# Shifting the layer norm and a convolution branch against a gated MLP's matmuls on one core

## The chip, the cores and the metric

The kernel runs on one core of one Trainium2 chip. The metric is device microseconds (us) of that core; lower is better. Five engines work side by side: TensorE (PE in the profile; PEld is its weight load), VectorE (DVE), ScalarE (ACT), GpSimd (POOL) and SyncE (SP), which issues most of the transfers.

## The reference, cut to what matters

The program computes a forward pass and all its gradients. `x` is 2048 x 1024 in bf16, normed row by row; the normed `xn` feeds two branches that are added.

```python
def _fwd_reference(...):
    def _A_ref(q, k, v, shift_k, ssm_k, ssm_D):          # the convolution branch
        k_shift = sum of k_pad[:, t:t + S] * shift_k[:, ks - 1 - t]   # ks = 4 taps per channel (a loop, condensed)
        kv = k_shift * v
        y = irfft(rfft(kv padded) * rfft(ssm_k padded))[:S]           # long convolution per channel, condensed
        y = y + kv * ssm_D
        return q * y
    def _B_ref(x, W_gate, W_up, W_down):                 # the MLP, F = 3584
        gate = x @ W_gate; up = x @ W_up                 # condensed
        h = relu(gate) * up
        return h @ W_down
    x = A_q
    xn = _layernorm(x)
    return x + _A_ref(xn, A_k, ...) + _B_ref(xn, B_W_gate, ...)

def reference(...):
    out, vjp = jax.vjp(_fwd_reference, ...)
    return (out, *vjp(grad_out))                         # 10 outputs
```

## The kernel before

The MLP's 512-column matmuls, "large" below, are the bulk of TensorE's work. The first phase, `hidden`, goes through fourteen blocks: seven blocks of weight columns for each half of the rows. The norm of the 16 row tiles is a generator that the first blocks advance by `chunk()`. The convolution branch is a second generator, `steps()`, with eight groups of 128 channels. The driver counts the planned nanoseconds of MLP work and advances the branch when its counter reaches zero: `A_START` sets when it begins, and each `yield n` says how much MLP work to lay between this step and the next.

```python
    a_steps, left = a.steps(), A_START            # A_START = 45_000
    for pace, phase in mlp():
        for ns in phase:                          # 1730 per group of 8 large matmuls
            left -= ns * pace
            while a_steps is not None and left <= 0:
                d = next(a_steps, None)
                ...
                left += d
```

The head of the branch loads the first group and writes a small table of the four taps to memory and back, to spread it over all partitions:

```python
    def steps(self):
        sk_t = self.shift_rows()          # taps transposed by TensorE
        self.pin = True
        nx = self.loads_1(0)              # hn (filter), gt (gradient), sD
        self.loads_2(nx)                  # kp (k), vt (v)
        yield 10000
        self.load(self.sk_d, sk_t[:])     # store of the tap table
        yield 13000
        self.load_taps(nx)                # reload into skb, one row for all partitions
        yield 9500
        self.load_xn(nx)                  # xt, the normed input
        ...
        for gi in range(self.NG):
            for p, d in self.slots(st, gi):   # p: TensorE's part, d: VectorE's
                self.run(p); self.run(d)
                yield self.SLOT               # 1760
```

A group's slots begin with the taps (`tk`: `ksh` and `tap` from `kp` and `skb`, on VectorE) beside the filter's first matmuls (`f1h`), then the product gt*xt, the flip of the filter (`flH`, a VectorE transpose) and its second matmuls (`f2H`):

```python
        tk = self.taps(st, ksh, kp, [(3, 0), (2, 1), (1, 2), (0, 3)])
        f1h = self.fwd1_filter(st)
        f1g = self.fwd1(st, "Bg", gt)
        yield f1h, tk if gi == 0 else None
        yield f1h, tk
        yield None, self.both(lambda: self.add_D(st), tk)
        yield None, (lambda: self.gate_grad(st)) if gi == 0 else tk
        yield None, tk
        flH = ...
        yield f1g, flH
        ...
```

In the MLP, what VectorE does after each product of the `up` weights frees the PSUM bank (TensorE's output buffer) for a later group, and stands in the same queue as the taps:

```python
                ps = self.ps_tile("ps_u")
                self.gemm8(ps, xT[s], wu, mid)
                self.pri.pin(nc.vector.scalar_tensor_tensor(out=ru[s][:, 1, :], ..., in1=ps[:], ...))
                self.pri.pin(nc.vector.tensor_tensor(out=ht[:], ...))
```

## Time and profile before

| | before |
|---|---|
| median, lowest and highest of 3 runs | 1912.05, 1912.03, 1914.49 us |
| the run that left the profile | 1915.21 us, span 1912.6 us, mean granted clock 0.998 |
| TensorE busy | 1898.4 us, 99% |
| the two waits of TensorE above 2 us | 3.18 us (copy of a tile), 2.14 us (gt*xt) |

A span runs from the core's first to its last instruction and is some 2 us shorter than the time.

One more view of before matters later, SyncE's timeline around the head of the branch (start, duration, instruction):

```profile
72.70 0.53 SPq L88 DMA_DIRECT2D sk_d<-sk_t  x1
...
73.77 4.45 SPq L88 DMA_DIRECT2D hn<-in_A_ssm_k_dram  x2
...
82.72 3.80 SPq L88 DMA_DIRECT2D kp<-in_A_k_dram  x4
86.56 1.40 SPq L88 DMA_DIRECT2D vt<-in_A_v_dram  x2
...
95.19 0.44 SPq L88 DMA_DIRECT2D skb<-sk_d  x1
```

The table's store goes out at 72.70, ahead of the group's own loads, which take SyncE from 73.77 to 87.96 only to issue; the reload goes at 95.19, and the first filter matmul is at 97.67 us. In the code the store is called behind the loads, but the program as built issues it in front of them, so the order of issue has to be read from the trace. In VectorE's timeline the first tap product then waits little for the table:

```profile
99.70 1.23 DVE L80 TENSOR_TENSOR ksh<-kp,skb 128x2048 bf16<-128x2048 bf16 x1 [0.72 <-DMA skb<-sk_d]
```

### The profile page before, as it was taken

The page shows a single profiled execution, that of the slowest core. Times are in us where ns is not written, and L with a number is a line of the kernel's source. Part 1 is how long each engine was busy: PE and PEld are TensorE (multiplying, and loading weights), DVE is VectorE, ACT ScalarE, POOL GpSimd, SP SyncE. Part 2 cuts the span into 40 slices and gives each one's busy share as a digit, 9 for nine tenths or more (in the row PEclk, how much of TensorE's full clock was granted, in tenths as well). Part 3 has the DMA queues.
Part 4 walks back from the last instruction along what each step waited for, and adds up shares of the span by engine and source line. Part 5 has one row for each costly group of instructions (what it writes and reads, how often), then busy time and mean ns, then how long its engine had stood idle before and what let it go on. Part 6 is the DMA issues. An engine that isn't in the chain of part 4 may idle for free.

```text
span 1912.6 us, 36039 instructions
## 1 busy us (share of the span) xinstructions
PE 1898.4 (99%) x15447; PEld 872.8 (46%) x15447; DVE 908.9 (48%) x1355; ACT 617.7 (32%) x858; POOL 15.0 (1%) x37
## 2 busy tenths in 40 slices
PE   8999999999999999999999999999999999999999
PEld 3444444444444444444444444444444544444444
DVE  6767767767767754543444444410122232222222
ACT  5854354354354344344344344311000000000000
POOL 1000000000000000000000000000000000000000
PEclk9999999999999999999999999999999999999999
DMA  9975688985784882655662633385999965555553
GB/s 244 264 190 147 171 189 185 221 191 135 182 192 134 248 232 78 171 134 183 159 172 80 174 100 122 102 244 184 255 246 239 231 159 121 121 121 121 121 121 72
DMA packets 692640, 323.13 MB, mean 169 GB/s; under 512 B 524024, under 2 KB 663040, under 8 KB 692480
## 3 DMA queue, kind: packets, MB, share of 16 engines
q1 hardware_dynamic: 681984, 299.99, 63.9%
q10 hardware_dynamic: 9216, 16.65, 2.9%
q0 software_dynamic: 1280, 4.20, 0.6%
q8 instruction: 120, 1.97, 0.4%
q14 instruction: 40, 0.33, 0.1%
HBM read 143.79 MB, written 95.44 MB: 125 GB/s over the span
## 4 chain that ended last, share of the span: by engine, by line
PE 97%; DMA 1%; DVE 1%; ACT 0%; SPq 0%; issue 0%; DVEq 0%; ACTq 0%
PE ps_x L1275 20%; PE ps_w L1048 20%; PE ps_u L799 10%; PE ps_h L799 10%; PE ps_o L1206 10%; PE ps_g L799 10%; PE ps_d L1048 9%; PE ps L72 6%; PE ps_d L1061 1%; PE ps_w L1061 1%; DMA ln_x<-in_A_q_dram 1%; DMA xt<-xn_d 0%; PE ps_r L1236 0%; DMA wu<-in_B_W_up_dram 0%; PE pst_x L831 0%; ACT ln_j L727 0%
## 5 line engine op out<-in xcount | busy, mean ns | idle before, releaser
L1048 PE MATMUL ps_w<-ugs,xn_nat 128*128 128x512 bf16 x1728 | 382.9, 379 | 0.0
L799 PEld LDWEIGHTS <-xnT 128*128 128x128 bf16 x1792 | 170.6, 98 | 214.9 <-issue 13.5
L1048 PEld LDWEIGHTS <-xn_nat 128*128 128x128 bf16 x1728 | 164.6, 98 | 200.6 <-issue 7.1
L799 PE MATMUL ps_g<-wg,xnT 128*128 128x512 bf16 x896 | 207.0, 382 | 3.9 <-DVE xnT L834 3.5
L799 PE MATMUL ps_u<-wu,xnT 128*128 128x512 bf16 x896 | 208.0, 382 | 0.2
L799 PE MATMUL ps_h<-wdT,goT 128*128 128x512 bf16 x896 | 205.6, 379 | 0.0
L1293 ACT ACTIVATE w<-xn,m 128x512 f32<-128x512 bf16 x32 | 24.3, 806 | 553.0 <-issue 317.2
L1275 PE MATMUL ps_x<-wgT,ggT 128*128 128x512 bf16 x896 | 198.6, 379 | 0.0
L1275 PE MATMUL ps_x<-wuT,guT 128*128 128x512 bf16 x896 | 198.6, 379 | 0.0
L1206 PE MATMUL ps_o<-wd,hT 128*128 128x512 bf16 (+1 forms) x896 | 187.6, 372 | 0.0
L1048 PE MATMUL ps_d<-g_nat,hs 128*128 128x512 bf16 x768 | 171.5, 379 | 0.0
L1275 PEld LDWEIGHTS <-guT 128*128 128x128 bf16 x896 | 87.7, 98 | 105.7
L1275 PEld LDWEIGHTS <-ggT 128*128 128x128 bf16 x896 | 87.7, 98 | 105.5
L1206 PEld LDWEIGHTS <-hT 128*128 128x128 bf16 x896 | 87.7, 98 | 100.0
L799 PEld LDWEIGHTS <-goT 128*128 128x128 bf16 x896 | 85.1, 98 | 104.1 <-issue 4.5
L302 DVE STREAM_TRANSPOSE flp<-C 128x1024 f32<-128x1024 f32 x48 | 90.4, 1932 | 84.9 <-ACT C L76 84.9
L902 DVE SCALAR_TENSOR_TENSOR ru<-ru,ps_u 128x512 bf16<-128x512 bf16 x112 | 76.5, 683 | 109.2 <-issue 37.1
L965 ACT CAST gh<-ps_h 128x512 bf16<-128x512 f32 x112 | 65.4, 584 | 178.4 <-PE ps_h L799 158.1
L76 ACT CAST C<-ps 128x1024 bf16<-128x1024 f32 x96 | 92.5, 1015 | 77.2 <-PE ps L72 76.3
L1152 ACT CAST wi<-ps_w 128x512 bf16<-128x512 f32 x108 | 63.8, 590 | 161.2 <-PE ps_w L1048 149.7
L1048 PEld LDWEIGHTS <-hs 128*128 128x128 bf16 x768 | 72.6, 98 | 89.5 <-issue 5.0
L1277 DVE CUSTOM_DVE_ANT_0 gx<-ps_x,gy 128x512 f32<-128x512 f32 x32 | 22.1, 691 | 182.1 <-PE ps_x L1275 182.1
(160 smaller groups left out, 1494.5 us busy)
## 6 DMA issues: line engine op xcount, KB each, us to landing
ug_d<-ru SPq DMA_DIRECT2D x112, 256.0 KB, 3.3
ugs<-ug_d SPq DMA_DIRECT2D x112, 256.0 KB, 5.1
wg<-in_B_W_gate_dram SPq DMA_DIRECT2D x56, 256.0 KB, 4.2
wu<-in_B_W_up_dram SPq DMA_DIRECT2D x56, 256.0 KB, 5.0
h_d<-ht SPq DMA_DIRECT2D x112, 128.0 KB, 2.3
hs<-h_d SPq DMA_DIRECT2D x56, 256.0 KB, 5.4
out_dram<-wi SPq DMA_DIRECT2D x56, 256.0 KB, 2.6
gt<-in_grad_out_dram SPq DMA_DIRECT2D x32, 256.0 KB, 5.0
```

The lines of the kernel that those rows point to most:

```text
L72: self.pri.pin(self.nc.tensor.matmul(out, lhsT=lhsT, rhs=rhs, start=start, stop=stop))
L76: self.pri.pin(self.nc.scalar.copy(out=out, in_=in_))
L302: self.pri.pin(self.nc.vector.transpose(out=df[:, c0:c0 + 32, :], in_=sf[:, c0:c0 + 32, :]))
L799: self.pri.pin(self.nc.tensor.matmul(ps[:], lhsT=xT[:, kt * P:(kt + 1) * P], rhs=w(kt), start=(kt == 0), stop=(kt == self.DT - 1)), always ...
L902: self.pri.pin(nc.vector.scalar_tensor_tensor(out=ru[s][:, 1, :], in0=ru[s][:, 0, :], scalar=0.0, in1=ps[:], op0=ALU.is_gt, op1=ALU.mult))
L965: self.pri.pin(nc.scalar.copy(out=gh[:], in_=ps[:]))
L1048: self.pri.pin(self.nc.tensor.matmul(ps[:], lhsT=lhsT(st), rhs=rhs(st), start=(st == 0), stop=(st == self.ST - 1)))
L1061: self.pri.pin(self.nc.tensor.matmul(ps[i][:], lhsT=lhsT(i, st), rhs=rhs(i, st), start=(st == 0), stop=(st == self.ST - 1)))
L1152: self.pri.pin(nc.scalar.copy(out=wo[0][:, d, :], in_=ps[:]))
L1206: nc.tensor.matmul(ps, lhsT=hT[:, kt, :], rhs=self.wd[:, kt, oc], start=(kt == 0), stop=(kt == self.FT - 1))
L1275: nc.tensor.matmul(ps, lhsT=T[:, kt, :], rhs=W[:, kt, oc], start=(i == 0), stop=(i == n - 1))
L1293: nc.scalar.activation(out=w[:, oc], in_=xn[:, oc], func=ACT.Identity, scale=m[:, 7:8], bias=m[:, 6:7])
```

## The change

Its intent is to take away TensorE's waits near the start. Part 1: the norm of tiles 6 and 7 goes behind the copies of tiles 4 and 5 in VectorE's queue. Part 2: the norm of tiles 12 to 15 moves to the second block, and so the whole branch starts later, since it needs all of xn. With it the first group's order is new, and the distances in the head of `steps()` are halved. Part 3: from group 3 on, the tail of a group carries the head of the next.

```diff
@@ steps(): the head of the branch
         nx = self.loads_1(0)
         self.loads_2(nx)
-        yield 10000
+        yield 5000
         self.load(self.sk_d, sk_t[:])
-        yield 13000
+        yield 5000
         self.load_taps(nx)
-        yield 9500
+        yield 7000
         self.load_xn(nx)
 ...
-A_START = 45_000
+A_START = 80_000
@@ slots(): the first group's order, and mixed borders (cut)
+    MERGED = 3
 ...
+        if gi == 0:
+            yield None, flH
+            yield None, flH
+            yield None, tk
+            yield f2H, tk
+            yield None, None
+            yield f2H, lambda: self.gate_grad(st)
+            yield f1g, None
 ...
+        if self.MERGED <= gi and not last:
+            nx = st["nx"]
 ...
+            self.begin(nx)
+            yield ib, nx["tk"]
+            yield nx["f1h"], nx["tk"]
 ...
@@ hidden(): the norm (cut)
+            def flip_ahead(sp):
+                flip(min(sp + 6, HS))
+                if sp == 0:
+                    with self.tc.issue_after(self.copied.ins):
+                        chunk()
 ...
                 yield from first_gate_up(2)
-                chunk()
 ...
-                if ahead and sp in (2, 4):
-                    chunk()
-                if n == 1 and sp < 4:
+                if n == 1 and sp in (0, 2):
+                    with self.tc.issue_after(self.stored.ins):
+                        load(8 + sp // 2)
+                if ahead and sp == 4 or n == 1 and sp != 2:
                     chunk()
```

## The prediction

> **What bounds the kernel now.** I read the page first, then the waits of TensorE, then the timeline around each of them, then busy time and clock by stretch. From the page:
>
> ```profile
> PE 1898.4 (99%) x15447; PEld 872.8 (46%) x15447; DVE 908.9 (48%) x1355; ACT 617.7 (32%) x858; POOL 15.0 (1%) x37
> PEclk9999999999999999999999999999999999999999
> ```
>
> TensorE is busy 1898.4 of 1912.6 us. The order listing of both kernels has the same instructions on every engine, form by form (30,896 rows on TensorE, 1,357 on VectorE, 892 on ScalarE, 1,043 on SyncE). So the change removes no work: what it can gain is TensorE's idle time, 1912.6 - 1898.4 = 14.2 us, and whatever TensorE loses while it counts as busy. The waits of TensorE (engine, line and releaser: us in total, times, longest):
>
> ```profile
> PE ps_g L799 <- DVE xnT L834: 3.5, 2, 3.2
> PE ps L72 <- DVE gt L80: 2.1, 1, 2.1
> PE pst_x L831 <- DVE ln_x L781: 1.7, 2, 1.5
> PE ps_warm L845 <- POOL warm L842: 1.5, 1, 1.5
> PE ps L72 <- ACT B L76: 0.9, 2, 0.5
> ```
>
> Two waits stand out: 3.2 us for the copy of a transposed tile, 2.1 us for the product of gradient and normed input. The 1.5 us waits belong to the start, which the change leaves alone, and some 2.6 us lie after the last matmul (it ends near 1910). The timeline shows both big waits and what follows them (start, duration, instruction, idle before it):
>
> ```profile
> 30.07 1.03 PE L799 MATMUL ps_h<-wdT,goT 128*128 128x512 bf16 x4
> 34.28 5.31 PE L799 MATMUL ps_g<-wg,xnT 128*128 128x512 bf16 x16 [3.18 <-DVE xnT L834]
> ...
> 109.80 0.61 PE L72 MATMUL ps<-gt,R 64*128 64x512 bf16 x4 [2.14 <-DVE gt L80]
> 110.33 5.31 PE L799 MATMUL ps_u<-wu,xnT 128*128 128x512 bf16 x16
> ```
>
> Sixteen matmuls after each wait take 5.31 us by the timeline; by the chain they take 5.31 and 5.25 where later groups of 16 take 3.45. So each wait is paid twice. The windows view (busy us, granted clock last but two) says why:
>
> ```profile
> 31.10:34.28 3.18, 0.00 (x0) 0.00 (x0) 2.48 (x7) 2.63 (x6) 0.00 (x0) 1.00 1.17 233
> 34.28:39.60 5.32, 5.32 (x17) 2.07 (x18) 3.02 (x10) 1.88 (x5) 1.07 (x2) 0.68 1.03 242
> 107.66:109.80 2.14, 0.00 (x2) 0.01 (x2) 1.29 (x2) 0.60 (x1) 0.00 (x0) 1.00 0.86 243
> 110.40:115.65 5.25, 5.25 (x19) 1.88 (x20) 3.94 (x5) 1.78 (x2) 0.00 (x0) 0.68 0.72 151
> ```
>
> The clock is whole during the idle stretch and 0.68 in the stretch after it: 5.32 us x (1 - 0.68) = 1.70 us lost.
>
> Why the first wait: VectorE's timeline.
>
> ```profile
> 28.30 0.42 DVE L904 TENSOR_TENSOR ht<-ru 128x512 bf16<-128x512 bf16 x1
> 31.73 0.17 DVE L745 TENSOR_SCALAR ln_b<-ln_s 128x2 bf16<-128x2 f32 x1 [3.02 <-ACT ln_j L727]
> 31.94 0.17 DVE L752 CAST ln_s<-ln_b 128x2 f32<-128x2 bf16 x1
> 32.14 0.88 DVE L756 TENSOR_SCALAR ln_x<-ln_x,ln_s 128x1024 bf16<-128x1024 bf16 x2
> 32.94 0.68 DVE L966 TENSOR_TENSOR ru<-ru,gh 128x1024 bf16<-128x1024 bf16 x1
> 33.55 1.28 DVE L834 COPY xnT<-pst_x 128x1024 bf16<-128x1024 bf16 x2
> ```
>
> VectorE idles 3.02 us in front of the norm of tiles 6 and 7, whose input lands late (the chain has that load from 22.30 for 7.13 us), while the copies of tiles 4 and 5 (their transposes run on TensorE from 29.18 for 1.06 us) stand behind it in the queue.
>
> **What the Trainium skill says.** "TensorE: Matmul & The Clock Gate", section "Part 1: The HAM clock gate": the clock is halved after an idle window of about 3.4 us, the window runs freely, and about 3.4 us of activity restores it. The trace agrees on the cost (1.7 us is half of 3.4) but not on the length: 2.14 us of idle were enough here, while 1.51 us at 8.3 us were not. The same page, "Architectural detail", says that VectorE and ScalarE work their queues strictly in order; the blocked copies are that. "Perfetto Trace Analysis", section "What 'DMA-bound' means", names an issuing sequencer that is solid DMA slices as one form of DMA limit; SyncE's timeline from 29.24 to 52.05 us is that, with gaps under 0.2 us.
>
> **The change part by part.** (1) In the changed order on VectorE the two copies of tiles 4 and 5 stand before the norm of 6 and 7, and on ScalarE the first evacuation of ps_h before its sums. Worked through with the durations above: ht ends 28.72; ps_h of the first tile ends about 28.4, its cast (0.58) about 29.0, the product 29.7, copies 30.4 and 31.0. TensorE comes to ps_g at 31.10. The 3.18 us go, and with them 5.31 - 3.45 = 1.86 us of slow clock: **-5.0**. The norm of 6 and 7 still hangs on the load (29.47), so it ends near 37.5 as before; TensorE now wants these tiles at 31.0 + 32 x 0.216 + 12 x 0.216 = 40.5. Covered by 3 us.
>
> (2) The convolution starts later: before, its first matmul stands behind 361 large matmuls, now behind 457, 96 x 0.216 = 20.7 us later by order. In group 0 the product gt*xt now has its place eleven slots after the load of xt (a slot is 8 large matmuls, 1.73 us), where it had four, about 7 us, against a load that the chain shows from 101.59 for 6.80 us. The second wait goes, 2.14 + (5.25 - 3.45): **-3.9**.
>
> (3) The norm of tiles 12 to 15 moves to the second block. xt needs all of xn. By counts, the last tile's scaling ends near 107 us, its store lands some 5.4 us later (the median of such stores from 22 to 70 us), and xt is issued near 97.67 + 20.7 - 5 = 113. Just covered; no gain in itself.
>
> (4) From group 3 on, the tail of a group carries the head of the next. A group then takes 544 or 560 large matmuls instead of 600, so the branch ends behind 5,025 large matmuls, not 5,057, in spite of the late start. The loads for the output phase come no later. Where the old group 4 began, two pairs of filter matmuls stood only 2 large ones apart at 682.9 us and waited 0.35 + 0.52 us for ScalarE; now they stand 16 apart: **-0.9**.
>
> (5) What it adds. In group 0 the second stage of the filter (f2H) comes one slot sooner, 64 large matmuls and 8 filter ones after the first: 64 x 0.216 + 2 x 0.54 = 14.9 us. VectorE's list up to the second flip, with its durations (5 tap operations of 1.22; two flips of 1.94; bias 0.54; two pairs of 0.69 and 0.42; two gradient products of 0.69) comes to 14.1 us, begins about 1.3 us after the first filter matmul and has about 0.5 us of gaps: 16.0. TensorE would wait 1 us: **+1.1**, too short to slow the clock, if 1.51 was.
>
> (6) After (1) TensorE comes 5 us sooner to the second block's weights. SyncE was issuing without a gap up to these, so their load will not move 5 us: I put it at 51.4 instead of 52.05 (one 0.4 us load no longer precedes it). With the median landing of 4.2 us and four issues over 2.7 us, pieces land from 55.6 to 58; TensorE wants them from 56.1 to 57.4. **+0.5**, an estimate between 0 and 1.5; likewise **+0.2** for tighter places in group 0 (the flip of the gradient and its second stage meet to within 0.2 us).
>
> Sum: -5.0 - 3.9 - 0.9 + 1.1 + 0.5 + 0.2 = -8.0. From the median, 1912.05 - 8.0 = **1904.0 us**, 0.4% less.
>
> **The rivals.** (a) The waits come back elsewhere: TensorE, 5 to 9 us ahead, meets late weights at 56 us (DMA share 0.99 to 1.07 of 16 engines from 48 to 60 us) or at the third block, and one gap of 2 us costs another 1.7 us of clock. For it: SyncE's gapless issue, and near 539 us a late weight load already costs about 0.7 us. Against it: the change takes one 512 KB load and four 256 KB stores of xn out of that stretch, and moves the convolution's first loads behind the third block's weights. If it wins at both places: 1907 to 1910. (b) VectorE becomes the bound in the mixed tails. Against it: before, VectorE is busy 36 of 50 us in the first phase but 19 to 26 in the second, and mixing begins at the seam between them, so even 10% more leaves half of it free. If wrong, a microsecond in each of five tails: 1909. (c) The whole 9 us plus the small waits go and nothing returns: 1902. (d) The later start pushes the branch past the output phase: +20 us, but the counts in (4) exclude it.
>
> **Range and chances.** Floor and ceiling are close: removing every idle microsecond and both slow stretches gives 1912 - 14.2 - 3.7 = 1894, so 2% (1873.8) is out of reach for a change without fewer instructions. The base runs lie within 2.5 us. Small returns are likelier than none, so the range leans up: 1901.0 to 1908.5. Faster by 2%: 0.01; same: 0.985; slower: 0.005.
>
> **What would show it.** Right: no wait of ps_g for xnT above 0.5 us, none of ps for gt, the granted clock whole after the first 7 us, TensorE's busy time down by about 3.7 us and idle by about 4.5. Step 5: a wait of ps for flp near 1 us around 128 us. Step 6: the first ps_g after 56 us waiting on wg. Wrong: a third slow stretch of the clock, or waits of TensorE on casts in the tails of groups 3 to 7, or a gap before the output phase.

## The result, and the profile after

The kernel after took 1914.96 us in the median of four runs (1913.69 to 1918.04), against 1912.17 (1912.03 to 1914.49) for before: ratio 1.0014, 95% interval 0.9997 to 1.0031. A ratio here is the mean time of one kernel's fast runs over that of the other's in the same rounds, so not quite the ratio of the medians quoted. Within 2%, "same" was right; the predicted gain of 8 us did not come, and the time lies above the range of 1901.0 to 1908.5.

The head of the page of after:

```profile
span 1911.9 us, 35799 instructions
...
PE 1879.4 (98%) x15217; PEld 872.8 (46%) x15447; DVE 909.8 (48%) x1355; ACT 618.3 (32%) x858; POOL 15.0 (1%) x37
```

It must not be read against before's 1898.4. This trace lacks 230 of the 15,447 matmul records, and the waits view lists 70 gaps of up to 0.2 us that "waited for nothing", where before's complete trace has none. The waits that have a releaser can be compared (engine, line and releaser: us in total, times, longest):

```profile
PE ps_g L835 <- DVE ru L939: 3.2, 1, 3.2
...
...
PE ps_g L835 <- DMA wg<-in_B_W_gate_dram: 0.7, 2, 0.5
PE ps_u L835 <- DMA wu<-in_B_W_up_dram: 0.6, 2, 0.3
```

Both big waits of before are gone. The wait for the tile copy is down to 0.3 us in the whole span, and in TensorE's timeline the product that had waited 3.18 us follows with no gap, at full speed:

```profile
30.30 3.62 PE L835 MATMUL ps_g<-wg,xnT 128*128 128x512 bf16 x15
```

The new waits lie together, 90 us later. TensorE's timeline there (the bracket is the idle time in front):

```profile
119.08 1.89 PE L835 MATMUL ps_g<-wg,xnT 128*128 128x512 bf16 x8
124.18 3.57 PE L835 MATMUL ps_g<-wg,xnT 128*128 128x512 bf16 x8 [3.21 <-DVE ru L939]
...
135.73 0.75 PE L72 MATMUL ps<-flp,FW 64*32 64x128 bf16 x64 [1.67 <-DVE flp L302]
```

Eight products take 1.89 us in front of the wait and 3.57 behind it. The windows view (us, busy times, then granted clock, DMA share, GB/s) shows why:

```profile
120.97:124.18 3.21, 0.00 (x1) 0.00 (x0) 1.84 (x3) 0.60 (x1) 0.00 (x0) 0.83 1.17 177
124.18:132.30 8.12, 8.12 (x25) 3.09 (x25) 8.04 (x10) 0.60 (x1) 0.00 (x0) 0.65 0.80 196
```

The clock is 0.65 over 8.12 us of work: 8.12 x 0.35 = 2.84 us lost. With the two waits that makes 3.21 + 2.84 + 1.67 = 7.7 us.

What TensorE waited for is an evacuation (`ru`), so the next view is VectorE's timeline:

```profile
113.59 0.43 DVE L941 TENSOR_TENSOR ht<-ru 128x512 bf16<-128x512 bf16 x1
122.31 1.23 DVE L80 TENSOR_TENSOR ksh<-kp,skb 128x2048 bf16<-128x2048 bf16 x1 [8.29 <-DMA skb<-sk_d]
123.45 0.68 DVE L939 SCALAR_TENSOR_TENSOR ru<-ru,ps_u 128x512 bf16<-128x512 bf16 x1
```

VectorE stands idle for 8.29 us in front of the first tap product, for the tap table (0.72 us in before). The evacuation that TensorE needs is next in the queue and cannot pass. And the table is late because of SyncE:

```profile
99.43 4.78 SPq L88 DMA_DIRECT2D hn<-in_A_ssm_k_dram  x2
...
109.12 4.52 SPq L88 DMA_DIRECT2D kp<-in_A_k_dram  x4
113.69 1.31 SPq L88 DMA_DIRECT2D vt<-in_A_v_dram  x2
...
115.91 0.56 SPq L88 DMA_DIRECT2D sk_d<-sk_t  x1
...
119.13 0.33 SPq L88 DMA_DIRECT2D skb<-sk_d  x1
```

The same eleven loads as before take 99.43 to 115.00 to issue, but now the table's store comes after them, at 115.91, and its reload at 119.13, when the store has landed. The first filter matmul is at 112.71, so the branch begins before its table has even been stored. In before the three yields laid 10 + 13 + 9.5 = 32.5 us of MLP work between the loads and the first slot; now it is 5 + 5 + 7 = 17 us, of which the issue alone eats 15.6.

### The profile page after: what moved, and what is told of

The parts are those of the page before. It is cut to its first block, busy times and chain, and to the rows that moved or that the text cites. A ratio compares the mean times of both kernels' runs of the same rounds, so it can differ in the third digit from the quotient of the medians.

```text
span 1911.9 us, 35799 instructions
## 1 busy us (share of the span) xinstructions
PE 1879.4 (98%) x15217; PEld 872.8 (46%) x15447; DVE 909.8 (48%) x1355; ACT 618.3 (32%) x858; POOL 15.0 (1%) x37
## 4 chain that ended last, share of the span: by engine, by line
PE 95%; DMA 2%; issue 1%; SPq 1%; DVE 1%; ACT 0%; DVEq 0%
PE ps_x L1319 20%; PE ps_w L1092 19%; PE ps_o L1250 10%; PE ps_u L835 9%; PE ps_h L835 9%; PE ps_g L835 9%; PE ps_d L1092 9%; PE ps L72 6%; PE ps_d L1105 1%; SPq L88 1%; PE ps_w L1105 1%; DMA wu<-in_B_W_up_dram 1%; DMA wg<-in_B_W_gate_dram 1%; PE ps_r L1280 0%; DVE flp L302 0%
## 5 line engine op out<-in xcount | busy, mean ns | idle before, releaser
L1092 PE MATMUL ps_w<-ugs,xn_nat 128*128 128x512 bf16 x1673 | 375.5, 379 | 5.7 <-issue 4.1
L1092 PE MATMUL ps_d<-g_nat,hs 128*128 128x512 bf16 x741 | 167.4, 379 | 3.2 <-issue 2.7
L835 PEld LDWEIGHTS <-goT 128*128 128x128 bf16 x896 | 84.9, 98 | 104.6 <-issue 5.7
```

The costliest lines, as they stand in the source:

```text
L835: self.pri.pin(self.nc.tensor.matmul(ps[:], lhsT=xT[:, kt * P:(kt + 1) * P], rhs=w(kt), start=(kt == 0), stop=(kt == self.DT - 1)), always ...
L1092: self.pri.pin(self.nc.tensor.matmul(ps[:], lhsT=lhsT(st), rhs=rhs(st), start=(st == 0), stop=(st == self.ST - 1)))
```

## The experiments

Eleven kernels ran (before and after again among them), all correct, each five times. The main theory (A) was that the late table in the head of the branch eats the gain. Its rivals, by the letters of the expectations: VectorE has too much work in group 0 whenever it starts (B), the loss lies in late weights for the second and third blocks (C), the gain of part 1 is eaten by late loads anyway (D), the mixed borders cost the time (E), the profile of before was of an unlucky run, so that there was less to gain (F).

| run | median (us) | ratio to before | 95% interval |
|---|---|---|---|
| after (first measured) | 1914.96 | 1.0014 | 0.9997 to 1.0031 |
| e1_taps_early | 1909.98 | 0.9987 | 0.9973 to 1.0001 |
| e2_taps_behind | 1908.52 | 0.9978 | 0.9966 to 0.9991 |
| e3_norm67_only | 1912.67 | 1.0004 | 0.9992 to 1.0017 |
| e4_no_mixing | 1915.5 | 1.0016 | 1.0004 to 1.0029 |
| b_again | 1912.77 | 0.9997 | 0.9985 to 1.0010 |
| a_again | 1916.02 | 1.0013 | 1.0000 to 1.0025 |
| e5_table_and_order | 1906.21 | 0.9963 | 0.9950 to 0.9975 |
| e9_conv_part_only | 1910.0 | 0.9982 | 0.9968 to 0.9995 |
| e10_cured_old_norm | 1907.83 | 0.9977 | 0.9963 to 0.9991 |
| e11_lead_restored | 1909.48 | 0.9986 | 0.9974 to 0.9999 |
| e12_cured_no_mixing | 1907.03 | 0.9971 | 0.9958 to 0.9983 |

Before, beside them, had medians of 1912.34 (the first four experiments), 1913.0 (the next four) and 1912.66 us (the last three).

**e1: the table early.** After, with the tap table stored and reloaded ahead of the group's loads.

```diff
+        yield 4000
+        self.load(self.sk_d, sk_t[:])
+        yield 4000
+        first = dict(gi=0)
+        self.load_taps(first)
         nx = self.loads_1(0)
+        nx.update(first)
         self.loads_2(nx)
-        yield 5000
-        self.load(self.sk_d, sk_t[:])
-        yield 5000
-        self.load_taps(nx)
+        yield 10000
         yield 7000
-A_START = 80_000
+A_START = 72_000
```

> Changed kernel with the tap table stored and reloaded ahead of the first convolution loads, all else as it was. Theory A (VectorE's queue stood 8.3 us behind the first tap product, which waited for the tap table; TensorE then waited 3.2 us for a bank, ran 6.8 us at half clock and waited 1.7 us for the flip): the 3.2 us wait and the slow stretch near 121 to 131 us go, VectorE's 8.3 us wait for the table falls under 1.5 us, a wait for the flip of about 1 us stays; time 1906 to 1909. Rival B (VectorE has too much to do in group 0 whenever it starts): waits of similar size stay, time 1913 or more. Rival C (the loss lies in late weights for blocks 2 and 3): VectorE's wait goes, time falls by less than 3 us.

It took 1909.98 us, 5.0 less than after though above the 1906 to 1909 expected, and the wait for the evacuation is gone. A smaller one of the same kind shows in VectorE's timeline:

```profile
117.01 1.23 DVE L80 TENSOR_TENSOR ksh<-kp,skb 128x2048 bf16<-128x2048 bf16 x1 [2.75 <-DMA kp<-in_A_k_dram]
```

With the table there, the tap product waits for `kp` instead, whose last issue SyncE ends only at 113.62. Then TensorE waits 2.3 us for the flip. So theory A holds, and the fault is wider than the table: the table and `kp` both stand near the end of a queue of issues that takes 16 us. Rival C, which allowed a gain of less than 3 us, falls.

**e2: the taps behind.** The table as late as in after, but the tap products traced behind the flips, so that nothing urgent stands behind them.

```diff
             if gi == 0:
+                yield f1h, None
+                yield f1h, None
+                yield None, lambda: self.add_D(st)      # was: tk in each of these and two more slots
 ...
             yield None, tk
+            yield None, tk
+            yield None, tk
             yield f2H, tk
-            yield None, None
-            yield f2H, lambda: self.gate_grad(st)
+            yield None, self.both(tk, tk)
+            yield f2H, self.both(tk, lambda: self.gate_grad(st))
```

> Changed kernel with the table as late as it was, but in group 0 the tap products traced behind the flips of the filter, so that nothing else on VectorE stands behind them. Theory A: the wait for the table itself is harmless when nothing urgent queues behind it, so the 3.2 us and 1.7 us waits and the slow stretch go here too; 1905 to 1909. Rival B (amount of work): the same instructions in the same group, so waits of 3 us or more return at the flips of the gradient or at the product of taps and v, 1911 or more. If the late table only moves the blockage, a wait for kvt near 150 us shows it.

It took 1908.52 us, 6.4 less than after. The table was as late, but no evacuation stood behind the tap product that needs it:

```profile
125.39 1.23 DVE L80 TENSOR_TENSOR ksh<-kp,skb 128x2048 bf16<-128x2048 bf16 x1 [0.58 <-DMA skb<-sk_d]
```

This separates two things that e1 changes at once: a late table costs TensorE next to nothing by itself, what costs is the place of its first user in VectorE's queue. A wait of 2.8 us for gt*xt came back, since that product now stood behind all seven tap operations.

**e3: part 1 alone.** Before, with only the norm of tiles 6 and 7 moved.

```diff
-                    self.gemm8(..., (lambda: flip(min(sp + 6, HS))) ...)
+                    self.gemm8(..., (lambda: flip_ahead(sp)) ...)     # flip, then chunk() after the copies
 ...
                 yield from first_gate_up(2)
-                chunk()
```

> Kernel before with only the first part of the change: norm of tiles 6 and 7 behind the copies of tiles 4 and 5. Everything else as before. My first step says -5.0 us (3.2 us of wait and 1.7 to 1.9 us of slow clock), so 1907 and no wait of ps_g for xnT above 0.5 us; the wait for gt*xt stays or grows to at most 4 us, as the load of xt does not come 5 us sooner with TensorE. Rival D (what is gained at the start is given back to DMA-bound loads by 110 us, because SyncE issues without gaps): the wait for gt*xt grows by about the 3.2 us gained, 1910 to 1912.

It took 1912.67 us, ratio 1.0004: no gain, though the wait was gone. The waits of TensorE say where it went:

```profile
PE ps_g L799 <- DMA wg<-in_B_W_gate_dram: 2.3, 3, 0.8
...
PE ps_u L799 <- DMA wu<-in_B_W_up_dram: 1.2, 2, 0.9
```

That is 3.5 us of late weights, 2.3 of it between 100 and 104.3 us at the third block, where before's timeline shows no such wait and b_again's 1.2 us in all. A slow stretch of the clock follows these waits (sixteen matmuls took 3.62 us at full speed, here ten take 4.00):

```profile
104.34 4.00 PE L799 MATMUL ps_g<-wg,xnT 128*128 128x512 bf16 x10 [0.77 <-DMA wg<-in_B_W_gate_dram]
```

So here theory D held in substance: a TensorE that comes earlier meets loads that do not. It met them at the weights, though, not at gt*xt as D had said: that wait went.

**e4: no mixing.** After with `MERGED = 8` for `MERGED = 3`.

> Changed kernel without the mixed borders: every group as long as the middle ones, so the branch ends behind 5,192 large matmuls instead of 5,024, with 184 left (39.7 us) before the output phase. Theory: mixing is worth 0.9 us at the old border plus whatever the output phase loses when its weights (29 us of load in the kernel before) start 36 us later: between 0 and 10 us slower than the changed kernel, a wait of ps_o for wd or hT. Rival E (mixing costs time through denser tails): this kernel is 1 us or more faster than the changed one.

It took 1915.5 us, as slow as after, with the same two waits in group 0 (3.6 and 2.8 us). From large matmul 2689 to 5300, which covers the borders, both kernels took 637.9 us. Rival E falls, and the mixing is worth nothing either.

**b_again: before, unchanged.**

> The kernel before once more, with a profile of its own. The profiled run of before took 1915.2 us against a median of 1912.2 and its granted clock was 0.998; most later runs of before have 1.000. Theory F (the slow stretches behind the two waits came with that one run, not with the kernel): this profile shows the waits of 3.2 and about 2 us with one slow stretch or none, its span is about 1910, and at least half of the runs have a mean clock of 0.9995 or more. Rival: a mean clock of 0.998 in most runs.

Again 1912.77 us, and its profile is of a run of 1912.05 us. TensorE's timeline at the two places where the prediction saw 3.18 and 2.14 us:

```profile
32.06 3.63 PE L799 MATMUL ps_g<-wg,xnT 128*128 128x512 bf16 x15 [1.44 <-DVE xnT L834]
...
108.12 0.61 PE L72 MATMUL ps<-gt,R 64*128 64x512 bf16 x4 [2.47 <-DVE gt L80]
108.66 5.30 PE L799 MATMUL ps_u<-wu,xnT 128*128 128x512 bf16 x15
```

The first wait is 1.44 us, not 3.18, and the matmuls behind it run at full speed (3.63 us, not 5.31). The second is there, with its slow stretch. Theory F is mostly right: of the 5.0 us that the prediction put on the first wait, this second profile has 1.4. The mean clocks say how common the slow stretches are: one of them costs some 1.7 us, or 0.0009 of the span, and of 32 later runs of before 16 have a mean of 1.000 (none), 15 have 0.999 (one) and a single one has 0.998, like the run that the prediction read.

**a_again: after, unchanged.**

> The changed kernel once more. If its slow stretch near 123 us belongs to the kernel, nearly every run has a mean clock of 0.998 to 0.999, the wait of ps_g behind VectorE near 121 us is 3 to 4 us again, and the median lies 2 to 3.5 us above before. If it was chance, the median comes down to 1912.

It took 1916.02 us, and the wait is not luck; it was longer:

```profile
PE ps_g L835 <- DVE ru L939: 6.4, 1, 6.4
```

VectorE idled 11.51 us for the table, because SyncE took 7.39 us to issue the two loads of `hn` (4.78 in after) and so stored the table at 118.55; the slow clock behind the wait lasted again 6.8 us. The mean granted clock was 0.998 in four of five runs, as in all four first runs of after; of the 32 runs of before in these three calls (b_again's among them), all but one had 0.999 or 1.000.

**e5: table early and order mended.** e1's head, and group 0 with the flips and gt*xt ahead of most of the taps.

```diff
             if gi == 0:
+                yield f1h, None
+                yield f1h, None
+                yield None, lambda: self.add_D(st)
 ...
             yield None, flH
             yield None, flH
             yield None, tk
-            yield f2H, tk
-            yield None, None
+            yield None, tk
             yield f2H, lambda: self.gate_grad(st)
-            yield f1g, None
-            yield None, None
+            yield None, tk
+            yield f2H, tk
+            yield None, tk
+            yield f1g, tk
+            yield None, tk
             yield f1g, None
```

> Changed kernel with the tap table early AND, in group 0, the tap products behind the flips with the product gt*xt ahead of five of the seven of them. Theory A, second part (what is left in the two cures is a wait for the flip of 2.3 us, because the load of kp also lands late, and a wait for gt*xt of 2.8 us behind all seven tap products): both go, no wait of TensorE above 0.8 us between 100 and 150 us, clock 1.000 in all runs; 1905 to 1907. Rival B (amount of VectorE work): the wait moves on to the flip of the gradient or to kvt, 1908 or more.

It took 1906.21 us (1905.64 to 1907.22), ratio 0.9963, faster than both kernels, with the clock at 1.000 in every run and no wait of TensorE above 0.3 us between 100 and 150 us. VectorE's first tap product has no idle time in front:

```profile
124.72 1.20 DVE L80 TENSOR_TENSOR ksh<-kp,skb 128x2048 bf16<-128x2048 bf16 x1
```

And in TensorE's timeline the second filter stage, which had waited 1.67 us in after, comes without a bracket:

```profile
126.73 0.75 PE L72 MATMUL ps<-flp,FW 64*32 64x128 bf16 x64
```

Against a_again, of the same rounds on the same chip, that is 1916.02 - 1906.21 = 9.8 us. Rival B falls too: VectorE has the same operations in group 0 and TensorE does not wait for them.

**e9: the convolution part only.** Before's norms with the branch of e1.

> Kernel before with only the convolution's part (later start with the tap table early, new order in group 0, mixed borders), the norms as before. If the parts are independent: the gt*xt wait of 2.1 us and the filter wait of 0.9 us go, the flip wait of 2.3 us comes: 0.5 to 1 us faster than before, the 3.2 us wait for xnT stays. If they need each other (rival D: the early norms' loads crowd the second block's weights whoever starts first): TensorE still reaches 56 us late because of the xnT wait, so the weights are in time, and the time is 1911 to 1912.

It took 1910.0 us, 3.0 less than before in its rounds where 0.5 to 1 was expected (its wait for the copy was 0.6 us, not 3.2); e1, which has the new norms as well, took 1909.98. In both, the tap product waits for `kp` (1.51 us of VectorE's time in e9) and TensorE for the flip (1.1 us). As long as that is so, the norm part adds nothing.

**e10: the cure with the old norm.** Before's norms with the branch of e5.

> The cured kernel of e5 (tap table early, product and flips ahead of the taps) with the norms of the kernel before. It gives the worth of the norm part where nothing gives it back: if the wait for xnT (1.4 us in the second profile of before, 3.2 in the first) is simply added, 1907.5 to 1909.5; if late weights of the second block eat the gain as in e3, the same as e5, 1905.5 to 1907.

It took 1907.83 us (0.9977) with a wait for the tile copy of 1.0 us and no slow clock. Against e5 that makes the norm part worth 1.6 us by the medians, or 0.0014 x 1912.7 = 2.7 us by the ratios. The intervals of the two overlap and the runs are of two chips, so this is a size, not a proof.

**e11: the lead restored.** After with the distances of before in the head. The table still follows the loads in the order of issue. Theory G: the short lead is the cause. Theory H: the place of the table behind the loads is, whatever the lead.

```diff
         self.loads_2(nx)
-        yield 5000
+        yield 10000
         self.load(self.sk_d, sk_t[:])
-        yield 5000
+        yield 13000
         self.load_taps(nx)
-        yield 7000
+        yield 9500
-A_START = 80_000
+A_START = 64_500
```

> The changed kernel with only the lead of the first convolution loads restored: traced 32.5 us ahead of the first slot as before, not 17, the first slot at the same place, the table's store still behind the loads in SyncE's order. Theory G (the fault is the shortened lead: 16 us of load issue do not fit in 17 us, so table and kp come after the first filter matmul): VectorE's wait for the table falls below 2 us, no wait of ps_g behind VectorE, a flip wait of 0.5 to 2 us, 1907 to 1910. Rival H (the order of the table behind the loads is what matters, as such): VectorE still waits over 5 us, 1913 or more. Rival C (the loads then crowd the third block's weights at 95 to 103 us): waits of ps_g or ps_u for wg or wu of 2 us or more.

It took 1909.48 us, 5.5 less than after. The tap product has no idle time in front and starts 1.2 us after the first filter matmul (116.12), the flip's wait is 0.4 us, and the clock is 1.000 in all five runs:

```profile
117.34 1.22 DVE L80 TENSOR_TENSOR ksh<-kp,skb 128x2048 bf16<-128x2048 bf16 x1
```

G holds and H falls. What it gives back, late weights as in C, is seen in the waits:

```profile
PE ps_u L835 <- DMA wu<-in_B_W_up_dram: 2.5, 3, 1.4
```

Of these, 2.3 us lie at 102 to 104.6 us, at the third block's weights: the branch's loads, early again, stand ahead of them in SyncE's queue, and the last of these weights is issued at 97.71 us where after had 95.63. This is a part of rival (a) of the prediction.

**e12: the cure without mixing.** e5 with `MERGED = 8`.

> The cured kernel of e5 without the mixed borders: the branch ends 168 large matmuls later. e4 against the changed kernel showed no difference beyond group 0 in the profiles. If mixing is worth nothing: 1905.5 to 1907; if it keeps the output phase's weights in time: 1908 or more with a wait of ps_o.

It took 1907.03 us, and the intervals of the two ratios overlap widely; the profiled spans even lie the other way (1903.6 us here, 1904.7 for e5). In a kernel without the stall, too, the mixing has no effect that these runs can see.

A twelfth kernel, late norms with the branch as early as before, was refused by the check before the chip: `xt` would be read before the last two tiles of xn are written (12.5% of xn undefined). So the late norms force the late branch and cannot be tried without it; the reverse is e9.

## Why the prediction was wrong

**What bounds the kernel: right.** TensorE's idle time and slow clock are all there was to move; the best kernel gained 0.37%. In e12, the same without mixing, whose trace is complete, TensorE is busy 1894.7 us of a span of 1903.6 us: 3.7 us less busy time than in before's profile and 5.3 us less idle time.

**Step 1, the tile copies, -5.0: right mechanism, wrong size.** The wait went (0.3 us left). But the 3.18 us and the slow stretch came from one run, 3.2 us slower than the median from which the gain was subtracted. The second profile has 1.44 us and no slow clock there, and nearly every later run of before has at most one slow stretch, where steps 1 and 2 together count two. The part alone gave 0 (e3), and some 2 us where nothing takes it back (e10 against e5).

**Step 2, gt*xt, -3.9: the wait went, but the change that removed it cost more than it gained.** "Eleven slots after the load of xt" was true, and after shows no wait for gt. The step looked only at the transfer whose wait it removed. The same lines of the diff that set that distance cut the lead of the first loads from 32.5 to 17 us, and the table and `kp` live on that lead. SyncE's 14.2 us of issues were on view in before's timeline, and the order listing had the table's store move from ahead of `hn` to behind the whole group. This is what made the prediction wrong: 7.7 us in the profile of after, up to 9.8 us in e5 against a_again. In the prediction's sum the false premise stands in step 5.

**Step 3, "Just covered; no gain in itself": right about xn,** since nothing waited for the late tiles. But `xt` was issued at 122.50, not near 113, behind the same loads; the eleven slots of step 2 covered the delay, not this step's reckoning. The care spent on that one landing was owed to the table's as well.

**Step 4, mixing, -0.9: the effect was put on the wrong cause.** The waits for ScalarE are gone in after, but in e4, without mixing, they are gone too: presumably the pairs of matmuls fall elsewhere because the branch starts later. Mixing itself is worth nothing measurable (e4, e12).

**Step 5, the flip, +1.1: here the premise failed.** The step lets VectorE's list begin "about 1.3 us after the first filter matmul". In after the first tap product began 122.31 - 112.71 = 9.6 us after it, for want of the table. The sum has no term for the 3.21 us of waiting and 2.84 us of slow clock that this cost. The wait for the flip that did come, 1.67 us, is what was left of that delay, so its nearness to 1.1 is luck. Where the premise holds, in e11 (1.2 us), the wait is 0.4 us: the list itself was sized well.

**Step 6, late weights, +0.5: not where it was placed.** At 55.37 us, the second block, TensorE did not wait: the weights were issued from 49.27, not 51.4, and landed in 4.7 us. The 0.7 + 0.6 = 1.3 us of late weights in after lie at 533 and 392 us.

**The rivals.** Rival (a), waits that come back elsewhere at 1907 to 1910 us, was the nearest, but it placed them at the weights. That is what e3, with 3.5 us, and e11, with 2.5, show; in after the return was in VectorE's queue, and larger. Rival (b) fell with e4. Rival (c) put 1902 us on "nothing returns"; e5, where almost nothing does, took 1906.2, so the gain to be had was nearer 7 us (0.0037 x 1912.7) than 10. Of what would show it wrong, "a third slow stretch of the clock" came as written, though in place of the first two and twice as long.

**The sum.** After lies 1914.96 - 1904.0 = 11.0 us above the prediction. The medians, of different chips, put 8.8 us of that (1914.96 - 1906.21) between after and e5, which has the same work, and 2.2 us between e5 and the prediction. The ratios, each against before in the same rounds, put it at (1.0014 - 0.9963) x 1912 = 9.8 us and 8.0 - 0.0037 x 1912 = 0.9 us. Either way most of it is the late table with what queued behind it, of which the profile of after shows 7.7 us in one place; that the rest is the mis-sized step 1 is likely but not shown.

What starts a slow stretch is not the length of the wait alone: waits of 2.14 us (before) and 2.47 us (b_again) were followed by one, waits of 2.3 us (e1) and 2.8 us (e2) were not. The packed traces hold the times at which the clock changes, and in each run these lie on a grid of 3.413 us; a slow stretch fills one or two windows of it. So the work that falls into one window was counted with the windows view. At full clock, windows with 0.00 to 1.30 us of TensorE work (before, b_again, after, a_again, e4) were followed by a slow one, and those with 1.37 us (a_again), 1.70 (after, e2) or more were not. The exception is e3, where 1.71 us in three pieces was followed by one. The grid cut e2's wait into 1.13 and 1.71 us. This is a pattern in 13 traces and not a proven rule; why all five runs of e2 kept a clock of 1.000 is not shown.

## What to carry to other kernels

When a change shortens the distance between loads and their first use, list every tile that the first use needs, with its place in the issuing engine's queue and the time of issue of all in front of it, not only the tile whose wait is to go. In an engine that works in order, put an operation whose input may be late behind those that free buffers for TensorE: e2 shows that this alone gives back 6.4 us with the input as late as ever. And before a wait is counted as a gain, see whether the profiled run is near the median, and whether a second profile has the same wait.

## What the Trainium skill lacked or had wrong

- "TensorE: Matmul & The Clock Gate", section "Part 1: The HAM clock gate", gives a free-running window of 3413 ns and a slow clock after an idle window of about 3.4 us. The slow stretches here fit the window: 3.41 us in b_again, 6.83 us in after and a_again. The idle length does not fit: 2.14 us of waiting were enough in before, 2.8 us in e2 were not. How much of a window must be idle is lacking; here the border lay between 1.30 and 1.37 us of work in a window of 3.41 us, with e3's 1.71 us as an exception.
- "DMA: Bandwidth & Descriptors", section "Issuing engines are not separate DMA queues", says that the time on the sequencer to initiate a DMA "is usually small relative to the DMA itself". Not here: the two loads of the filter, 256 KB each, took SyncE 4.78 us to issue, 2.4 us each on average against a median of 7.4 us from issue to landing, and the group's eleven loads took 15.6 us of issuing. Figures for the issue time by shape and by load on the DMA engines are lacking: the same two loads took 7.39 us in a_again.
- No page gives what the store and dependent reload of a small table cost together when other transfers fill the engines: here 6.4 us from the store's issue at 115.91 to the first use at 122.31, for a table of 8 KB (32 x 128 in bf16) that the reload spreads to 128 KB, at a DMA share of 0.96 to 1.17.
- "Perfetto Trace Analysis" has nothing on how far one profiled run stands for a kernel (1915.21 us against a median of 1912.05), nor on missing matmul records (230 of 15,447 in after, which leave 70 false gaps of up to 0.2 us in the waits view).
